# The last two batches' gate and val products by seven block products instead of eight, in a fused sigmoid attention and SwiGLU kernel

## The chip, the cores and the metric

The kernel runs on one core of one Trainium2 chip. TensorE multiplies matrices out of SBUF into PSUM (eight banks of 128 x 512 fp32), ScalarE (ACT) applies functions, VectorE (DVE) does arithmetic on tiles, GpSimd (POOL) casts and issues some transfers, and SyncE (SP) issues most of them. Each engine works its instructions in order; semaphores tie the engines together. The metric is the time on the device in microseconds (us), lower is better.

## What is computed

Eight batches of attention with 12 heads of 448 positions and 64 columns, where a sigmoid takes the place of the softmax, and then a SwiGLU block on the 3584 resulting rows of 768 columns:

```python
scores = scale * q @ k.T - log(S)            # per batch and head, S = 448
attn = 1 / (1 + exp(-scores))
x = (attn @ v)  -> rows (batch, position), 12 * 64 = 768 columns
g = x @ w_gate                               # 768 x 1536
val = x @ w_val                              # 768 x 1536
out = (g * sigmoid(g) * val) @ w_out         # 1536 x 768
```

Inputs and outputs are fp32; the kernel works in bf16 and fp16 with fp32 sums.

## The kernel before

**Attention.** 24 steps `i`: three groups of four heads for each of eight batches. For each step q, k and v are loaded by SP (`load`, 448 KB each), cast by GpSimd, q and k transposed by a transfer (`tr_dma`, from step 6 on) into a `qkT` tile, of which there are three. `burst` computes a pair of score tiles, `sig` the sigmoid of each on ScalarE into a `pt` tile, and `pv` the product with v, seven pairs a step. VectorE copies its result into `xT` tiles (two 128 x 448 tiles a step, six a batch).

**First FFN product (`f1`).** For each batch and each of 12 column blocks of 128, the gate and the val product: six 128 x 128 blocks of weights against six `xT` tiles. Two column blocks are worked together, each weight block as four 64 x 64 quarters (`quarters`, L511), so that different quarters of the array work on different products. ScalarE takes the sigmoid of gate, VectorE multiplies twice and puts the result into `hT` (two batches a tile), and with that frees the banks.

**Second FFN product (`f2_set`, `f2_pair`, `f2_single`).** It takes two batches together (pair `m`, 0 to 3), in sets of two blocks of 128 rows; each set is already worked by seven block products in place of eight. The sums of weight blocks that this needs are formed once (`weight_sums`). Two products are worked together in quarters while the steps go on; after them they are worked whole (`f2_single`, L678).

**What sets the order.** The kernel doesn't leave the order to the framework. Every piece of work is recorded as an `Op` with an engine, an assumed duration, what it depends on, and the buffers that it takes and gives. `list_schedule` (L70) then plays these through and gives each engine the order in which its instructions are written: on each engine the first operation that is ready among the next ones in the recorded order (40 for TensorE and VectorE, 30 for ScalarE, 8 for GpSimd, 1 for SP, so SP keeps the recorded order). A buffer ring is ready when the user of its slot before is done, by the planner's clock. For transfers that clock adds the assumed times on one common queue, and 1.7 us for the landing (`LAT["SP"]`). The order is fixed when the kernel is built; on the chip each engine waits wherever its next instruction isn't ready.

The recording loop (L872) goes through the steps and four slots in each. It hands out `f1` column blocks by `nf` (about four a step, behind attention by `LAG`), and `f2` items by `f2acc` (12.5 / 22 a slot). Loads for step i+3 are issued behind the transposes for step i+2. What is left of `f1` and `f2` when the steps are over is worked in a row.

Of the kernel before, what the change touches and what calls it, by code (L numbers as in the profile page):

```python
# [9 lines left out]
FP32 = mybir.dt.float32  # L10
FP16 = mybir.dt.float16
BF16 = mybir.dt.bfloat16
COPY = mybir.ActivationFunctionType.Copy
SIGM = mybir.ActivationFunctionType.Sigmoid
MULT = mybir.AluOpType.mult
ADD = mybir.AluOpType.add
SUB = mybir.AluOpType.subtract
# [10 lines left out]
class Op:  # L28
# [3 lines left out]
    def __init__(self, eng, dur, fn, deps=(), mode=("F", "F"), take=(), give=(), desc=(0, 0)):  # L32
        self.eng, self.dur, self.fn, self.mode = eng, dur, fn, mode
        self.deps = [d if isinstance(d, tuple) else (d, 0.0) for d in deps if d is not None]
        self.take = [Slot(t) for t in take]
        self.give = list(give)
        self.rank = self.t0 = self.t1 = None
        self.first = False
        n, size = desc
        self.hold = n == 1792  # L40
        self.dma = 2.0 if n == 1792 else n / 16 * max(0.042, size / 22300 - 0.003)
# [13 lines left out]
LAG = 1  # L55
# [8 lines left out]
TURN = "ACT"  # L64
WO = 4
MARGIN = 1.0
FREE = {"P"}


def list_schedule(ops, bufs, window):  # L70
# [113 lines left out]
def kernel(  # L184
# [10 lines left out]
    nc = tc.nc  # L195
# [19 lines left out]
    ctx.enter_context(tc.manual_schedule())  # L215

    slots = {"A": 2, "P": 8, "st": 11, "src": 2,
             "v16": 3, "qkT": 3, "pt": 10, "xT": 14, "osb": 3, "osf": 4, "S": 2, "t1": 3, "s16": 2}

    idn = one.tile([128, 128], BF16, tag="idn", name="idn")  # L220
    sb_t = one.tile([128, 1], FP32, tag="sbiast", name="sbiast")
# [33 lines left out]
    def op(*a, **kw):  # L255
        o = Op(*a, **kw)
        ops.append(o)
        return o

    def bank(name, n=0):  # L260

        return psum.tile([128, 512], FP32, tag=f"P{R['now'].got('P')[n].n}", bufs=1, name=name)

    def cp(eng, o, i):
        if eng == "ACT":
# [177 lines left out]
    def sig(key, dep, slot):  # L443
        def fn(a):
            def go():
                if a == 0:
                    T[("pt",) + key] = sb.tile([128, 2, S], FP16, tag="pt", bufs=slots["pt"], name="pt")
                nc.scalar.activation(out=T[("pt",) + key][:, a], in_=T[("sc",) + key][a][:, 0:S], func=SIGM, bias=sbias,  # L448
                                     scale=qkscale)
            return go  # L450
        x = op("ACT", 0.44, fn(0), deps=[dep], take=["pt"], give=slot[1:2])
        R["pt ring", key] = x.take
        R["sig"] = R[("pt",) + key] = op("ACT", 0.44, fn(1), deps=[x and (x, LAT["ACT"] + LATE)], give=slot[:1] + slot[2:])

    def pv(i):

# [72 lines left out]
    def f1(b, f):  # L529

        two = (f, f + 1)
        m, o = divmod(b, 2)

        def both(w, nm, parts, p):
            def fn():
                if p == 0:
                    for n, x in enumerate(two):
                        T[nm, b, x] = bank("ps_" + nm, n)[:, 0:S]
                quarters([[(T[nm, b, x], w[x // FC][:, j, (x % FC) * 128:(x % FC + 1) * 128], T["xT", b, j]) for x in two]
                          for j in range(*parts[p][1:])], parts, p, (nm, b, f))  # L540
            return fn

        def fs(f):
            def fn():
                t = T["s16", b, f] = sb.tile([128, S], FP16, tag="s16", bufs=slots["s16"], name="s16")
                nc.scalar.activation(out=t, in_=T["g", b, f], func=SIGM)  # L546
            return fn

        def ft(f):
            def fn():  # L550
                t = T["t1", b, f] = sb.tile([128, S], FP16, tag="t1", bufs=slots["t1"], name="t1")
                nc.vector.tensor_tensor(out=t, in0=T["g", b, f], in1=T["s16", b, f], op=MULT)  # L552
            return fn

        def fh(f):
            def fn():
                if o == 0 and f == 0:
                    T["hT", m] = sb.tile([128, NF, 2 * S], FP16, tag="hT", bufs=2, name=f"hT_{m}")
                nc.vector.scalar_tensor_tensor(  # L559
                    out=T["hT", m][:, f, o * S:(o + 1) * S], in0=T["v", b, f], scalar=HSC,  # L560
                    in1=T["t1", b, f], op0=MULT, op1=MULT)
            return fn
        xs = [(R["xT", b, j], 0.19 * j) for j in range(KC)]
        old = R["f2", m - 2] if m >= 2 and b % 2 == 0 else []

        def joint(w, nm, deps):
            a = None
            parts = [(0, 0, KC), (1, 0, KC)]
            if (b, f) == (0, 0) and nm in SPLIT:
                parts = [(0, 0, 4), (1, 0, 4), (1, 4, KC), (0, 4, KC)]  # L570
            ws = [(x, 0.38 * n) for c in {x // FC for x in two} for n, x in enumerate(R["w16", "w" + nm, c])]
            for p, (t, j0, j1) in enumerate(parts):
                same = p and parts[p - 1][0] == t
                a = op("PE", 0.19 * (j1 - j0), both(w, nm, parts, p), mode=("Q", "Q"), take=[] if p else ["P", "P"],
                       deps=[(x, 0.19 * n) for n, (x, _) in enumerate(xs[j0:j1])] + deps + ws +
                       [a and ((a, LAT["PE"] + LATE) if same else turn(a, (nm, b, f, p - 1)))])
                banks = banks if p else a.take
            return a, banks
        g, gbank = joint(wg16, "g", [])
        ts = []  # L580
        for n, x in enumerate(two):
            s = op("ACT", 0.45, fs(x), deps=[g], take=["s16"])
            s.first = 2
            ts.append(op("DVE", 0.54, ft(x), deps=[s], take=["t1"], give=s.take + gbank[n:n + 1]))

        def val():
            v, vbank = joint(wv16, "v", old + [(g, 1.0)])
            if f == NF - 2:
                v.give += [x for o, _ in xs for x in o.take]
            for n, (x, t) in enumerate(zip(two, ts)):  # L590
                R["hT", b, x] = op("DVE", 0.54, fh(x), deps=[v, t] + old, give=vbank[n:n + 1] + t.take)
        return val

    def weight_sums():

# [264 lines left out]
    def f1_step(b, f):  # L860
# [4 lines left out]
        if b % 2 == 1 and f == NF - 1:  # L865
            f2q.extend(f2_items(b // 2))

    f2acc = 0.0
    wsums = weight_sums()
    next(wsums)  # L870
    fpos = 0
    for i in range(NQ + QB + 2):  # L872
        att = i < NQ
        for sl in range(4):
            if i < QB:
                nf = 0
            elif i < QB + 4:
                nf = 1 if sl < 3 else 0
            else:
                nf = min(2, max(0, 4 * (i - QB) + sl - LAG - fpos + 1))  # L880
            if i < NCW and sl == 3:
                cast_wc(i)
            if WO < i <= WO + 4 and sl == 1:
                for f in range(3 * (i - WO - 1), 3 * (i - WO)):
                    cast_wo(f)
            if i > WO + 5 or i == WO + 5 and sl > 1:
                for _ in range(WSN):
                    next(wsums, None)
            f1s = []
            while len(f1s) < nf and fpos < B * NF and ("xT", fpos // NF, KC - 1) in R:  # L890
                f1s.append(divmod(fpos, NF))
                fpos += 1
            later = bursts(i, sl)
            for ds in later[:1 if i >= SPREAD else 2]:
                burst(ds)
            if sl == 0 and QB < i <= NQ:
                pv(i - 1)
            if sl == 0 and 0 < i < QB:
                pv(i - 1)
            if sl == 3 and i == QB - 1:  # L900
                pv(i)
            if att and i + 1 < NPE and sl in (1, 2):
                tr_pe(i + 1, sl - 1)
            for b, f in f1s:
                f1_step(b, f)
            for ds in later[1:] if i >= SPREAD else []:
                burst(ds)
            if att and sl == 0 and i + 2 < NQ:
                casts(i + 2)
            if att and sl == 1 and NPE <= i + 2 < NQ:  # L910
                tr_dma(i + 2)
            if sl == 1:
                if AHEAD <= i + 3 < NQ:
                    loads(i + 3)
                if WO <= i < WO + 4:
                    for f in range(3 * (i - WO), 3 * (i - WO + 1)):
                        load_wo(f)
                    uses[1] = uses[0]
            f2acc = f2acc + 12.5 / 22.0 if f2q else 0.4
            while f2q and f2acc >= f2q[0][0] and ("ws", 4, NH - 2) in R:  # L920
                w, fn = f2q.pop(0)
                f2acc -= w
                fn(not att)
    while fpos < B * NF:
        b, f = divmod(fpos, NF)
        fpos += 1
        f1_step(b, f)
    while f2q:
        f2q.pop(0)[1](True)

    window = {"PE": 40, "ACT": 30, "DVE": 40, "POOL": 8, "SP": 1}
    end = 0.0
# [39 lines left out]
```

## Time and profile before

| | |
|---|---|
| three runs | 406.99, 407.3, 410.8 us, median 407.3 |
| span of the profiled execution, first to last instruction | 407.6 us (0.3 above the median of the runs) |
| TensorE busy | 400.1 us, 98% |
| VectorE busy | 230.0 us, 56% |
| ScalarE busy | 223.2 us, 55% |
| GpSimd busy | 132.7 us, 33% |
| granted TensorE clock, mean | 0.997 of full speed |
| last score product of attention | about 333 us |
| whole output products at the end | 375.7 to 403.2 us |

The page shows the busy time of each engine, the span in 40 slices with the busy share of each in tenths, the transfers, the chain of work that ended last, and the groups of instructions that cost most. PE is TensorE, PEld its weight loads, DVE VectorE. A line like `L522 PE MATMUL ps_g<-xT,wg 64*64 64x448 x2304` is a group: source line, engine, the tile written and the tiles read, the shape, and how many. The time between matmuls is read from the chain in order of time rather than from their busy time, since matmuls overlap in the array.

### The profile page before, as it was taken

To read this page: it belongs to the slowest core of one execution; us is meant where nothing else is said; L and a number is where in the kernel's file an instruction comes from. 1 tells how busy PE (TensorE), PEld (TensorE's weight loads), DVE (VectorE), ACT (ScalarE), POOL (GpSimd) and SP (SyncE) were. 2 spreads that over 40 slices of the span, in tenths; PEclk is the share of its full clock that TensorE was granted. 3 is DMA by queue.
4 is the path that set the end of the run, shared out by engine and by line. 5 is a ranking of instruction groups with operands and counts; after the bars stand their busy time and mean duration, and the time that the engine had idled before them with its cause. 6 is when DMAs were issued, how large, how long until landed. Compare 5 with 4: busy or idle time off the path is not lost.

```text
span 407.6 us, 17541 instructions
## 1 busy us (share of the span) xinstructions
PE 400.1 (98%) x7871; PEld 306.8 (75%) x7873; DVE 230.0 (56%) x420; ACT 223.2 (55%) x472; POOL 132.7 (33%) x194
## 2 busy tenths in 40 slices
PE   8999999999999999999999999999999999999995
PEld 3446667668998787665679888889989898997663
DVE  2624544447795467553564664745465656546874
ACT  4997677757767743377647456475474552121100
POOL 1888855656454221522332322422310200000000
PEclk9999999999999999999999999999999999999998
DMA  7999999999676609455665564663500303010335
GB/s 268 380 376 376 376 277 318 304 320 264 184 185 183 160 26 203 139 129 108 209 183 92 172 136 143 177 133 122 124 4 3 80 2 77 7 42 18 101 85 148
DMA packets 64795, 67.58 MB, mean 166 GB/s; under 512 B 35536, under 2 KB 60880, under 8 KB 64720
## 3 DMA queue, kind: packets, MB, share of 16 engines
q1 hardware_dynamic: 62864, 59.78, 51.6%
q0 software_dynamic: 1536, 6.29, 6.0%
q8 instruction: 61, 1.00, 1.0%
q10 hardware_dynamic: 320, 0.39, 0.3%
q14 instruction: 14, 0.11, 0.1%
HBM read 47.19 MB, written 11.01 MB: 143 GB/s over the span
## 4 chain that ended last, share of the span: by engine, by line
PE 95%; ACT 2%; DMA 1%; issue 1%; DVE 0%; ACTq 0%
PE ps_v L522 27%; PE ps_g L522 27%; PE ps_o L522 16%; PE ps_sc L427 8%; PE ps_pv L468 7%; PE ps_o L678 7%; ACT pt L448 2%; PE ps_warm L818 1%; PE ps_tr L384 1%; DMA st<-in_q_dram 1%; DVE st L687 0%; DVE src L268 0%; ACTq L504 0%
## 5 line engine op out<-in xcount | busy, mean ns | idle before, releaser
L448 ACT ACTIVATE pt<-ps_sc 128x448 f16<-128x448 f32 x336 | 162.7, 550 | 77.8 <-PE ps_sc L427 77.3
L522 PE MATMUL ps_v<-xT,wv 64*64 64x448 f16 x2304 | 136.2, 349 | 0.0
L522 PE MATMUL ps_g<-xT,wg 64*64 64x448 f16 x2304 | 134.6, 349 | 0.8 <-issue 0.6
L522 PEld LDWEIGHTS <-wg 64*64 64x64 f16 x2304 | 93.7, 107 | 22.2 <-issue 2.4
L522 PEld LDWEIGHTS <-wv 64*64 64x64 f16 x2304 | 93.2, 107 | 21.2 <-issue 1.4
L552 DVE TENSOR_TENSOR t<-ps_g,s 128x448 f16<-128x448 f32 x96 | 56.5, 618 | 71.6 <-ACT s L546 71.6
L546 ACT ACTIVATE s<-ps_g 128x448 f16<-128x448 f32 x96 | 48.1, 545 | 59.0 <-PE ps_g L522 50.0
L559 DVE SCALAR_TENSOR_TENSOR hT<-ps_v,t 128x448 f16<-128x448 f32 x96 | 55.4, 618 | 43.4 <-PE ps_v L522 26.2
L427 PE MATMUL ps_sc<-qkT 64*64 64x448 bf16 x672 | 77.2, 354 | 0.1
L270 POOL CAST src<-st 128x896 bf16<-128x896 f32 (+1 forms) x43 | 40.8, 951 | 64.5 <-DMA st<-in_q_dram 35.8
L270 POOL CAST v<-st 64x448 f16<-64x448 f32 (+1 forms) x72 | 41.5, 577 | 60.0 <-PE ps_pv L468 42.5
L522 PEld LDWEIGHTS <-hT 64*64 64x64 f16 x1080 | 52.2, 107 | 7.0 <-issue 0.2
L522 PE MATMUL ps_o<-wo,hT 64*64 64x384 f16 x648 | 49.2, 323 | 0.0
L522 PE MATMUL ps_o<-st,s 64*64 64x384 f16 x480 | 45.7, 323 | 0.0
L468 PE MATMUL ps_pv<-pt,v 64*64 64x448 f16 x672 | 45.3, 350 | 0.1
L522 PE MATMUL ps_o<-st,hT 64*64 64x384 f16 x432 | 41.2, 323 | 0.0
L427 PEld LDWEIGHTS <-qkT 64*64 64x64 bf16 x672 | 33.7, 107 | 9.9 <-issue 1.6
L687 DVE SCALAR_TENSOR_TENSOR osb<-ps_o,osb 128x384 f32<-128x384 f32 x63 | 32.9, 550 | 10.4 <-PE ps_o L522 6.6
L268 DVE CAST xT<-ps_pv 128x448 f16<-128x448 f32 x40 | 23.6, 617 | 25.0 <-PE ps_pv L468 25.0
L697 POOL DMA_DIRECT2D out_dram<-osb x32 | 16.7, 526 | 59.0 <-DVE osb L687 59.0
L468 PEld LDWEIGHTS <-v 64*64 64x64 f16 x672 | 26.6, 107 | 9.1 <-issue 2.7
L522 PEld LDWEIGHTS <-s 64*64 64x64 f16 x480 | 29.1, 107 | 3.8 <-issue 0.4
(44 smaller groups left out, 212.8 us busy)
## 6 DMA issues: line engine op xcount, KB each, us to landing
st<-in_q_dram SPq DMA_DIRECT2D x24, 448.0 KB, 5.0
st<-in_v_dram SPq DMA_DIRECT2D x24, 448.0 KB, 6.6
st<-in_k_dram SPq DMA_DIRECT2D x23, 448.0 KB, 5.9
out_dram<-osb POOLq DMA_DIRECT2D x32, 192.0 KB, 3.3
st<-in_moe_w_gate_dram SPq DMA_DIRECT2D x12, 384.0 KB, 8.8
st<-in_moe_w_val_dram SPq DMA_DIRECT2D x12, 384.0 KB, 8.8
st<-in_moe_w_out_dram SPq DMA_DIRECT2D x12, 384.0 KB, 7.6
out_dram<-st SPq DMA_DIRECT2D x16, 192.0 KB, 2.8
```

What stands on the lines that cost most here:

```text
L268: nc.vector.tensor_copy(out=o, in_=i)
L270: nc.gpsimd.tensor_copy(out=o, in_=i)
L427: nc.tensor.matmul(out=sc[a][64 * (g ^ a):64 * (g ^ a) + 64, 0:S].rearrange("k (s p) -> k s p", s=NS), lhsT=kT[r, s, 64 * g:64 * g + 64], ...
L448: nc.scalar.activation(out=T[("pt",) + key][:, a], in_=T[("sc",) + key][a][:, 0:S], func=SIGM, bias=sbias, scale=qkscale)
L468: nc.tensor.matmul(out=T["pv", i, a][64 * g:64 * g + 64, :], lhsT=T["v16", i][r, a, s, :], rhs=T["pt", i, s][r, a, :], start=(s == 0), sto ...
L522: mm = nc.tensor.matmul(out=o[cs], lhsT=w[rs, cs], rhs=x[rs], start=p == 0 and k == 0, stop=p == len(parts) - 1 and k == len(steps) - 1)
L546: nc.scalar.activation(out=t, in_=T["g", b, f], func=SIGM)
L552: nc.vector.tensor_tensor(out=t, in0=T["g", b, f], in1=T["s16", b, f], op=MULT)
L559: nc.vector.scalar_tensor_tensor(out=T["hT", m][:, f, o * S:(o + 1) * S], in0=T["v", b, f], scalar=HSC, in1=T["t1", b, f], op0=MULT, op1=MULT)
L678: nc.tensor.matmul(out=T["p", m, k, n], lhsT=lhs()[:, x // 2, x % 2], rhs=rhs(x), start=x == 0, stop=x == NH - 1)
L687: nc.vector.scalar_tensor_tensor(out=c(*dst), in0=T["p", m, k, n], scalar=HREC, in1=c(*other), op0=MULT, op1=ADD)
L697: dma.dma_start(out=out[rows, cols].rearrange("(p s) d -> s p d", s=NS)[s], in_=T[("osb",) + t][64 * x:64 * x + 64, cols])
```

## The change

Batches 6 and 7 (pair 3) leave `f1`. Once the last attention step is recorded, their gate and val products are worked by six sets, one for each pair of column blocks (f, f + 6), by seven products of half the inner size in place of eight. Each product is a whole 128 x 128 tile times three, not in quarters.

- `f1_sums` forms four combinations of weight blocks for each set and for gate and val by VectorE, from step 13 on, one such group every third slot. All groups use one buffer (`TT`). `store` writes each to DRAM from SP; it is recorded when the next group is.
- `wload` brings them back after attention into the staging buffers, five ahead.
- `xsum` forms combinations of `xT` tiles by VectorE when attention is done.
- `one_set` issues the seven products for gate and val in turn. Results that several outputs share stay in the bank, and ScalarE takes a copy (`snap`) between two products that add onto it. SILU by ScalarE takes the place of the sigmoid and one multiplication. All SILUs come behind the last sigmoid.
- The ring of `qkT` tiles has two in place of three; `pt` has 9, now handed out by the planner in any order, and `xT` 16 in place of 14.
- The first six batches' `f1` blocks are handed out at four a step up to nine steps past the third, then at 3.2; `f2` items at 0.42 a slot (0.6 after the last `f1` block). Two items of pair 2 are recorded after each set, the last three behind the sets.

```diff
-FREE = {"P"}
+FREE = {"P", "pt", "W"}
+NPLAIN = 6
+RATE = 0.42
+FR = 3.2
+F0 = 9
+RATE2 = 0.6
+KEEP = 3
+TW0 = 13
+TSTEP = 3
+MIX = 2
...
-             "v16": 3, "qkT": 3, "pt": 10, "xT": 14, "osb": 3, "osf": 4, "S": 2, "t1": 3, "s16": 2}
+             "v16": V16, "qkT": 2, "pt": PT, "W": NEARLY0, "TT": 1, "xT": XT, "osb": 3, "osf": 4, "S": 2, "t1": 3, "s16": 2}
...
+    def f1_sums(nm, f):
+
+        w = wg16 if nm == "g" else wv16
+        t = []
+
+        def q(k):
+            return t[0][:, k]
+
+        def fn(k, x, y):
+            def go():
+                if k == 0:
+                    t.append(sb.tile([128, 4, NC, 128], FP16, tag="TT", bufs=1, name=f"tt_{nm}{f}"))
+                nc.vector.tensor_tensor(out=q(k), in0=x(), in1=y(), op=SUB)
+            return go
+        b = {(r, c): (lambda r=r, c=c: blk(w, f, r, c)) for r in range(2) for c in range(2)}
+        ws = [x for c in (f // FC, (f + NH) // FC) for x in R["w16", "w" + nm, c]]
+        o = [op("DVE", 0.36, fn(0, b[0, 1], b[0, 0]), deps=ws, take=["TT"])]
+        o.append(op("DVE", 0.36, fn(1, b[1, 1], lambda: q(0)), deps=[o[0]]))
+        o.append(op("DVE", 0.36, fn(2, b[1, 1], b[0, 1]), deps=[o[1]]))
+        o.append(op("DVE", 0.36, fn(3, b[1, 0], lambda: q(1)), deps=[o[2]]))
+
+        def store():
+            R["T", nm, f] = [op("SP", 0.5, lambda: nc.sync.dma_start(
+                out=tsum[NH * "gv".index(nm) + f], in_=t[0].rearrange("p k j f -> p (k j f)")), deps=[o[3]],
+                give=o[0].take, desc=(128, 4 * NC * 256))]
+        return store
...
+        def wload(nm, f):
...
+            old = [R["cq", NQ - 1][-1], R["ck", NQ - 1][-1]] + [R["v16", i] for i in (NQ - 2, NQ - 1)]
+            WS[k] = op("SP", 0.5, fn, deps=old + R["T", nm, f], take=["W"], desc=(128, 4 * NC * 256))
...
+                for j in range(NC):
+                        nc.tensor.matmul(out=T["fp", key], lhsT=win(nm, f, n)()[:, j], rhs=xin[n](j),
+                                         start=n in first and j == 0, stop=j == NC - 1,
+                                         skip_group_check=n not in first)
...
+            both(1, lambda nm: [last] if last else [R["xT", b1, j] for j in range(KC)])
+            for nm in "gv":
+                snap(nm, 1)
+            both(2)
+            add("g", 0, 0, 2, 1, True)
+            silu(0, 0)
+            both(6, lambda nm: [C[nm, "s", 1]])
+            for nm in "gv":
+                snap(nm, 6)
+            add("v", 0, 0, 2, 1, True)
+            fin(0, 0)
+            both(5)
+            both(7, lambda nm: [C[nm, "s", 6]])
+            for nm in "gv":
+                snap(nm, 7)
+            add("g", 1, 1, 5, 7, False)
+            silu(1, 1)
+            add("v", 1, 1, 5, 7, False)
+            both(4, lambda nm: [C[nm, "s", 7]])
+            silu(1, 0)
+            fin(1, 0)
+            fin(1, 1)
+            both(3, lambda nm: [C[nm, 1, 1]])
+            add("g", 0, 1, 3, 6, True)
+            silu(0, 1)
+            add("v", 0, 1, 3, 6, True)
+            fin(0, 1)
+            return P["v", 7]
...
+            if i >= TW0 and (4 * i + sl) % TSTEP == 0:
+                if tstores:
+                    tstores.pop()()
+                if tpairs:
+                    tstores.append(f1_sums(*tpairs.pop(0)))
...
-            while len(f1s) < nf and fpos < B * NF and ("xT", fpos // NF, KC - 1) in R:
+            while len(f1s) < nf and fpos < NPLAIN * NF and ("xT", fpos // NF, KC - 1) in R:
...
-            f2acc = f2acc + 12.5 / 22.0 if f2q else 0.4
-            while f2q and f2acc >= f2q[0][0] and ("ws", 4, NH - 2) in R:
+            f2acc = f2acc + (RATE2 if fpos == NPLAIN * NF else RATE) if f2q else 0.4
+            while len(f2q) > (KEEP if fpos == NPLAIN * NF else 0) and f2acc >= f2q[0][0] and ("ws", 4, NH - 2) in R:
                 w, fn = f2q.pop(0)
                 f2acc -= w
-                fn(not att)
-    while fpos < B * NF:
...
+                fn(False)
+            if i == NQ and sl == 3:
+                sums, wload, one_set = f1_pair(B // 2 - 1)
+                sums()
+                todo = [(nm, f) for f in range(NH) for nm in "gv"]
+                for x in todo[:5]:
+                    wload(*x)
+                last = None
+                for f in range(NH):
+                    last = one_set(f, last)
+                    for _ in range(min(MIX, len(f2q) - KEEP)):
+                        f2q.pop(0)[1](False)
+                    for x in todo[5 + 2 * f:7 + 2 * f]:
+                        wload(*x)
     while f2q:
-        f2q.pop(0)[1](True)
+        f2q.pop(0)[1](False)
+    for _, fn in f2_items(B // 2 - 1):
+        fn(True)
```

## The prediction

> **What bounds the kernel now.** I read in the order: the page's busy shares and slices, the chain of work that ended last, the stretches of time, then the queue of transfers.
>
> ```profile
> PE 400.1 (98%) x7871; PEld 306.8 (75%) x7873; DVE 230.0 (56%) x420; ACT 223.2 (55%) x472; POOL 132.7 (33%) x194
> ...
> PE   8999999999999999999999999999999999999995
> ...
> PE 95%; ACT 2%; DMA 1%; issue 1%; DVE 0%; ACTq 0%
> ```
>
> TensorE is the chain: 95% of it, and busy in every slice but the first and the last. So a product that goes is worth its own time, and any wait that TensorE gets is a loss of the same size. Nothing else is near a limit by its share (VectorE 56%). What a product costs stands in the chain in order of time, near the end (start, length, what):
>
> ```profile
> 371.13 1.14 PE ps_g L522 x24
> 372.26 1.14 PE ps_v L522 x24
> 373.40 1.08 PE ps_o L678 x6
> 374.48 1.26 PE ps_v L522 x24
> 375.74 27.42 PE ps_o L678 x168
> ```
>
> 24 quarter matmuls are six 128x128 weight blocks over 448 columns: 1.136 us, 0.1893 us a block. 168 whole matmuls of 384 columns take 27.42 us, 0.1632 each, so 0.1904 for 448 columns. A change between quarters and whole tiles costs 1.08 - 6 x 0.163 = 0.10 us one way and 1.26 - 1.14 = 0.12 us back, 0.11 on average.
>
> [...]
>
> **Part 1, products removed.** Batches 6 and 7 now take 2 batches x 12 column blocks x 2 (gate, val) x 6 = 288 blocks in quarters, 288 x 0.1893 = 54.5 us. After: 6 sets x 2 x 7 products x 3 = 252 whole blocks, 252 x 0.1904 = 48.0 us. Gain 6.5 us, all on the chain.
>
> **Part 2, mode changes.** In the order built from the changed kernel the last stretch (after attention) changes between quarters and whole tiles 23 times, because half pairs of output products fill the gaps of the sets; before it is 3 times. 20 x 0.11 = 2.2 us lost.
>
> **Part 3, work around the new sets.** A set costs TensorE 14 x 0.57 = 8.0 us. ScalarE: 6 snapshots and 4 SILUs at 0.55 us (the sigmoid rows, 550 and 545 ns) = 5.5 us. VectorE: 7 reads of PSUM at 0.62 us and 3 products in SBUF at about 0.35 = 5.4 us. Both are covered by TensorE. Tightest step: product 7 of gate ends, 0.2 us to ScalarE, snapshot 0.45 to 0.55, 0.15 back, and product 4 of gate stands 1.1 us behind product 7 (val's lies between): 0.2 to 0.3 us to spare. If that cover is gone it costs at most some 1 us a set, 6 us in all; I take 0.3 us for the part. The 12 sums of xT blocks lie under 8.1 us of products. The table load (row: ACT_TABLE_LOAD 1283 ns) lies in the 2.5 us in which ScalarE waits for product 2. The reloads from DRAM are issued a set ahead. The tail is the same.
>
> So far: -6.5 + 2.2 + 0.3 = -4.0 us.
>
> **Part 4, the weight sums during attention.** 48 subtractions of 128x384; the row L664 of 128x768 takes 0.55 us, so between 0.28 (half) and 0.42 (the 128x512 copy); I take 0.33, 16 us of VectorE in some 110 us. VectorE is busy 7.5 us of each 13 there now (nine stretches from 141 to 259 us): room enough. But the four blocks of a set share one buffer (`TT`, one slot): the first subtraction of each set waits until the *store of the set before has landed*, and VectorE stops in order until then. Queued behind it are the reads that free PSUM banks (`t1`, `hT`, `osb`), and TensorE waits for those.
>
> When does the store land? It is issued on SP behind the transpose and three loads. With two qkT buffers, transpose i+2 waits for the last score product of step i (before, with three, of step i-1; its qkT is wanted a step of 13 us later and lands in 4 to 7.5, so that itself costs nothing). So end of scores, transpose, q, k, v, store. Stretch 150 to 285 us (queue view: size, median time to landing), and one such turn:
>
> ```profile
> st<-in_q_dram SPq DMA_DIRECT2D x8, 448.0 KB, 4.3
> st<-in_k_dram SPq DMA_DIRECT2D x8, 448.0 KB, 5.4
> st<-in_v_dram SPq DMA_DIRECT2D x8, 448.0 KB, 6.2
> qkT<-src SPq DMA_TRANSPOSE x9, 5.8
> ```
>
> ```profile
> 220.22 3.82 SPq L410 DMA_TRANSPOSE qkT<-src  x1
> 224.09 0.59 SPq L300 DMA_DIRECT2D st<-in_q_dram  x1
> 224.72 0.49 SPq L300 DMA_DIRECT2D st<-in_k_dram  x1
> 225.26 0.47 SPq L300 DMA_DIRECT2D st<-in_v_dram  x1
> ```
>
> Here v is issued 5.0 us after the transpose and lands 6.5 later: 11.55 us. The eight turns from 154 to 270 us give 12.1, 8.3, 12.0, 9.5, 11.55, 9.7, 9.1, 10.85. Add 0.3 from the last score to the transpose's issue, 1.0 for 384 KB more in the queue (consecutive w_out loads land 1.0 apart) and 0.1 to wake VectorE: the store lands 9.7 to 13.5 us after the step's last score, mean 11.8. The kernel's planner believes 9.3 (transpose 2.5 us, loads 1.24 each, store 1.08, landing 1.7, from its constants), and puts the waiting subtraction there: in the built order it stands just behind reads of products that end 8 to 9 us after that score.
>
> How late may it start? I walked the built order: for each of these waits, the first TensorE instruction whose semaphore needs a VectorE instruction queued behind it, its distance (sum of products, in the times above) from the step's last score, less the VectorE work between (0.33, 0.6 and 0.51 us each) and 0.15 us. Example, val sums of block 0: last score at 155.0 us of product time, score product 4940 at 166.5 needs `t1` behind one subtraction (latest start 165.4), and the pv product at 167.8 needs `hT` behind four (165.1). Allowance 10.1 us. Eight waits stand so, with allowances of 10.1, 9.8, 10.5, 10.0, 10.5, 10.2, 10.2 and 10.5 us. The other three wait for stores issued behind no loads; they have 0 to 0.3 us too little, 0.5 us in all.
>
> Landing less 10.2: 3.3, 0, 3.2, 0.7, 2.8, 0.9, 0.3, 2.1, mean 1.7 us a wait. With the four turns before 150 us (emptier queue: 1.0, 0, 0.2, 1.2) it is 1.3. Eight waits: 10 to 13 us; I take 10.5 + 0.5 = 11 us. Bounds: all turns like the shortest, 0; all like the longest, 8 x 3.3 + 1.5 = 28. TensorE doesn't get it back: it has no idle time to give. In 150 to 285 us of before the VectorE reads end a median 1.3 us ahead of the TensorE instruction that needs them, and one unforeseen wait of 1.5 us at 170 us cost nothing; that speaks for the lower half of 0 to 28.
>
> [...]
>
> **Sum.** 407.6 (span of the profiled execution) - 4.0 + 11 = 414.6 us. The median of the three runs is 407.3, 0.3 below that span: 414.3.
>
> **Rivals.** *A, forecast: the products go, the store's wait takes more back*, 408 to 422 us. For it: eight turns of which seven exceed the allowance. Against: transfers in the after run may be less crowded, since output products come slower (fewer stores from POOL in each turn).
>
> *B, the waits are harmless: faster.* Stores land by about 10 us as in the turns of 8.3 and 9.1 us, or banks have more to spare than the walk says. 407.3 - 4.0 = 403.3, down to 401 if the mode changes hide behind other waits. For: the harmless wait at 170 us. Decides below some 0.4 us a wait.
>
> *C, waits eat just the gain*: 0.3 to 1 us a wait, 403 to 411 us, within 1%.
>
> *D, transposes late*: with two qkT buffers a score burst waits for its transpose. Landing 4 to 7.5 us of a 13 us step leaves over 5 us; it decides only if the turn before slips by that. If it did, 1 to 2 us in each of 18 steps: 425 to 440. Unlikely.
>
> **Chances.** A with D: slower by over 1% (above 411.4 us) 0.60; C: within 1% 0.25; B: faster by over 1% (below 403.2) 0.15. One per cent is about what a measurement of this kernel can tell from no change. Range 402.5 to 422: from B, less the 0.3 us of part 3 and some of the mode changes, to eight waits of 2.2 us each (the mean of the six longest turns): 407.3 - 4.0 + 17.4 + 0.5 = 421.2.
>
> **What would show it.** Right: from 150 us on, VectorE's subtractions idle 1 to 3 us each for the DMA of `tsum`, about eleven times; the slices of TensorE between the 14th and the 28th drop from 9 to 8; attention's last score comes 8 to 13 us later than the products alone allow; the last stretch has whole products at 0.19 us a block without gaps, and some 23 mode changes. Wrong: subtractions that wait as long while TensorE shows no idle time (banks to spare), or that hardly wait (stores land sooner); or gaps between the products of a set, ahead of product 7 or 4, waiting for ScalarE.

## The result, and the profile after

The changed kernel takes 421.51 us (median of four runs, 419.89 to 424.62), the kernel before 408.14 beside it: 1.033 times the time, 95% interval 1.027 to 1.039. The forecast was 414.3 us, slower, with a range of 402.5 to 422. The time lies just inside the range. The direction and the mechanism were right and the size was not: 7 us more were forecast and 13.4 came.

The page of the changed kernel, the lines that answer to those shown of before:

```profile
span 422.8 us, 15909 instructions
...
PE 401.5 (95%) x6973; PEld 267.4 (63%) x6973; DVE 249.9 (59%) x492; ACT 244.5 (58%) x509; POOL 134.6 (32%) x202
...
PE   8999989999999999998979898699999999999995
...
PEclk9999999999999999999989999879999999999999
...
PE 72%; DMA 13%; DVE 6%; SPq 4%; ACT 3%; issue 1%; DVEq 0%; ACTq 0%
```

TensorE was the chain with 95%; now it holds 72%, and transfers 13%. Its slices fall below 9 between the 19th and the 26th, which is 190 to 275 us, inside the stretch in which the waiting groups of weight sums are made (181 to 303 us). After that it is full again. The granted clock, which I hadn't thought of, falls too, in the 21st, 26th and 27th slice.

What ends VectorE's idle time before a group's first subtraction, between 150 and 320 us (us in total, times, longest):

```profile
DVE tt_g L640 <- DMA tsum<-tt_v: 14.3, 4, 6.8
DVE tt_v L640 <- DMA tsum<-tt_g: 12.1, 5, 4.0
```

So the first subtraction of a group of sums stands nine times for the store of the group before, 26.4 us in all. VectorE in order of time (start, length, ..., idle time before it and what ended it), the two worst:

```profile
212.45 0.59 DVE L640 TENSOR_TENSOR tt_v<-wv,wv 128x384 f16<-128x384 f16 x1 [3.96 <-DMA tsum<-tt_g]
...
274.50 0.55 DVE L640 TENSOR_TENSOR tt_g<-wg,wg 128x384 f16<-128x384 f16 x1 [6.81 <-DMA tsum<-tt_v]
```

TensorE in order of time, just behind each:

```profile
214.73 1.71 PE L492 MATMUL ps_pv<-pt,v 64*64 64x448 f16 x16 [2.53 <-DVE osb L908]
...
275.57 0.59 PE L449 MATMUL ps_sc<-qkT 64*64 64x448 bf16 x4 [4.96 <-DVE osb L908]
```

The wait doesn't stop TensorE by itself. It stops the read of a bank (`osb`) queued behind the subtraction, and TensorE waits for that bank: a pause of 2.53 us stands behind the wait of 3.96, and one of 4.96 behind that of 6.81.

**Where the 13.4 us come from.** I count, for each matmul, its start less the sum of the spacings of all matmuls before it (the rows of the prediction: 0.0473 us for a quarter of 448 columns, 0.1904 for a whole one, and so on). While TensorE runs without a gap this number stands still; what it grows by is lost. From 120 us to attention's last score product it grows by 1.3 us in the kernel before and by 20.3 in the changed one: 19.0 lost. From there to the end it grows by 0.2 and by 2.5: 2.3 for the mode changes. The products that went are worth 6.5. That is 407.6 - 6.5 + 2.3 + 19.0 = 422.4, against a span of 422.8.

The last stretch went as forecast. The chain in order of time there (start, length, what):

```profile
333.10 2.07 PE ps_o L546 x48
335.17 0.67 PE ps_g L723 x3
335.85 0.57 PE ps_v L723 x3
336.42 0.57 PE ps_g L723 x3
```

A product of three blocks takes 0.57 us without a gap behind it. Where the mode changes it takes 0.67, and 48 quarters of 384 columns take 2.07 in place of 48 x 0.0406 = 1.95: 0.10 and 0.12 us a change.

### The profile page after: what moved, and what is told of

Same layout as the page of the kernel before. It is cut to its first block, busy times and chain, and to the rows that moved or that the text cites. A ratio compares the mean times of both kernels' runs of the same rounds, so it can differ in the third digit from the quotient of the medians.

```text
span 422.8 us, 15909 instructions
## 1 busy us (share of the span) xinstructions
PE 401.5 (95%) x6973; PEld 267.4 (63%) x6973; DVE 249.9 (59%) x492; ACT 244.5 (58%) x509; POOL 134.6 (32%) x202
## 4 chain that ended last, share of the span: by engine, by line
PE 72%; DMA 13%; DVE 6%; SPq 4%; ACT 3%; issue 1%; DVEq 0%; ACTq 0%
PE ps_v L546 15%; PE ps_g L546 13%; PE ps_o L546 12%; DMA tsum<-tt_v 7%; PE ps_o L899 7%; PE ps_g L723 6%; PE ps_pv L492 6%; PE ps_sc L449 6%; PE ps_v L723 6%; DMA tsum<-tt_g 5%; ACT pt L470 2%; SPq L322 2%; SPq L432 2%; PE ps_warm L1039 1%; DVE tt_v L640 1%
## 5 line engine op out<-in xcount | busy, mean ns | idle before, releaser
L546 PE MATMUL ps_v<-xT,wv 64*64 64x448 f16 x1728 | 102.6, 354 | 0.0
L546 PE MATMUL ps_g<-xT,wg 64*64 64x448 f16 x1728 | 99.2, 349 | 1.5 <-issue 1.1
L546 PEld LDWEIGHTS <-wv 64*64 64x64 f16 x1728 | 63.1, 109 | 23.8 <-issue 1.5
L546 PEld LDWEIGHTS <-wg 64*64 64x64 f16 x1728 | 61.7, 107 | 25.1 <-issue 3.1
L576 DVE TENSOR_TENSOR t<-ps_g,s 128x448 f16<-128x448 f32 x72 | 42.9, 618 | 44.6 <-ACT s L570 44.4
L918 POOL DMA_DIRECT2D out_dram<-osb x40 | 20.8, 525 | 115.2 <-DVE osb L908 105.5
L583 DVE SCALAR_TENSOR_TENSOR hT<-ps_v,t 128x448 f16<-128x448 f32 x72 | 41.7, 617 | 23.7 <-PE ps_v L546 16.7
L570 ACT ACTIVATE s<-ps_g 128x448 f16<-128x448 f32 x72 | 36.5, 548 | 24.2 <-PE ps_g L546 18.2
L449 PEld LDWEIGHTS <-qkT 64*64 64x64 bf16 x672 | 30.4, 107 | 23.4 <-issue 13.5
L908 DVE SCALAR_TENSOR_TENSOR osb<-ps_o,osb 128x384 f32<-128x384 f32 x70 | 36.6, 549 | 8.3 <-PE ps_o L546 7.9
```

What stands on the lines that cost most here:

```text
L449: nc.tensor.matmul(out=sc[a][64 * (g ^ a):64 * (g ^ a) + 64, 0:S].rearrange("k (s p) -> k s p", s=NS), lhsT=kT[r, s, 64 * g:64 * g + 64], ...
L546: mm = nc.tensor.matmul(out=o[cs], lhsT=w[rs, cs], rhs=x[rs], start=p == 0 and k == 0, stop=p == len(parts) - 1 and k == len(steps) - 1)
L583: nc.vector.scalar_tensor_tensor(out=T["hT", m][:, f, o * S:(o + 1) * S], in0=T["v", b, f], scalar=HSC, in1=T["t1", b, f], op0=MULT, op1=MULT)
L908: nc.vector.scalar_tensor_tensor(out=c(*dst), in0=T["p", m, k, n], scalar=HREC, in1=c(*other), op0=MULT, op1=ADD)
```

## The experiments

All edits are to the changed kernel, but for the memsets, which go into the kernel before. The waits are read from 120 us on. The growth is the number above, from 120 us to attention's last score. "Half clock" is the time between 100 and 380 us in which the granted clock is 0.5.

| run | VectorE's waits for a store, us | growth, us | half clock, us | time, us |
|---|---|---|---|---|
| before | - | 1.3 | 0 | 407.4 to 408.4 |
| the change | 26.4 | 20.3 | 10.2 | 421.5 |
| one group of sums | 0 | 1.3 | 0 | 403.7 |
| belief +2 us | 9.7 | 5.7 | 0 | 408.3 |
| belief +4 us | 0 | 4.8 | 0 | 409.2 |
| store from ScalarE's queue | 11.1 | 13.4 | 3.4 | 416.7 |
| one group a step, from step 10 | 32.6 | 25.9 | 10.2 | 427.4 |
| two slots | 21.4 | 18.0 | 6.8 | 420.2 |
| three `qkT` tiles | 23.4 | 17.7 | 6.8 | 421.3 |
| belief +4 us, one group a step, from step 10 | 3.9 | 2.4 | 0 | 404.3 |

**One group of sums: what the rest of the change is worth.** The other eleven groups and their stores are left out; every reload takes the first group.

```diff
-                nc.sync.dma_start(out=T["W", nm, f].rearrange("p k j f -> p (k j f)"), in_=tsum[NH * "gv".index(nm) + f])
+                nc.sync.dma_start(out=T["W", nm, f].rearrange("p k j f -> p (k j f)"), in_=tsum[0])
...
-            WS[k] = op("SP", 0.5, fn, deps=old + R["T", nm, f], take=["W"], desc=(128, 4 * NC * 256))
+            WS[k] = op("SP", 0.5, fn, deps=old + R["T", "g", 0], take=["W"], desc=(128, 4 * NC * 256))
...
-    tpairs = [(nm, f) for f in range(NH) for nm in "gv"]
+    tpairs = [("g", 0)]
```

> The changed kernel with eleven of the twelve groups of weight sums and their stores left out; every reload after attention takes the one group that is formed (so the products of batches 6 and 7 use wrong sums). What is left is the price of the seven products, the mode changes, the rings and the hand-out rates. Theory: -6.5 us of products, +2.2 of mode changes, +0.3: 403 to 405 us, and TensorE without a pause from 100 us on. Rival (transposes a step later, or the slower hand-out, cost by themselves): 410 us or more.

403.71 us against 407.39 of the kernel before, ratio 0.991 (95% interval 0.988 to 0.993, here and below): 3.7 us won, where the prediction's parts 1 to 3 came to 4.0. The loss lies in the sums and their stores.

**The planner's belief.** The planner counts a store as landed 1.7 us after its place in the common queue of transfers. Here it adds 4.0 us for these stores alone. The instructions are the same, and only their order changes.

```diff
+        self.late = 0.0
...
-                    o.t1 = dma + LAT["SP"]
+                    o.t1 = dma + LAT["SP"] + o.late
...
+            R["T", nm, f][0].late = 4.0
```

> The changed kernel with one thing altered: the planner believes that each store of a weight-sum group lands 4 us later than before. The work is the same; VectorE's subtractions are merely written later in its order. Theory (VectorE waits for the store's landing, TensorE pays, and its clock halves in the longer pauses): VectorE's idle time for the stores falls from 26 us to below 6, TensorE's loss between 190 and 310 us from 19.5 us to below 4, and the time from 421.5 to 403 to 407 us. Rival (the loss comes from 16 us more work on VectorE and from the transposes issued a step later, and the waits are only where it shows): 415 us or more.

409.16 us, ratio to before 1.004 (1.002 to 1.007). The page:

```profile
PE   8999999999999999999999999999999999999995
...
PEclk9999999999999999999999999999999999999999
```

No subtraction waits for a store any more, and the dips of TensorE and of its clock are gone: 12 of the 13.4 us come back. It misses the expected 403 to 407. Attention's growth is 4.8 us in place of the 1.3 with one group of sums, and behind attention's last score there are 31 mode changes in place of 23 and the growth is 4.9 in place of 2.5. The last group's sums come only at 293 us; that this is what costs the rest is not shown by this run.

With 2.0 in place of 4.0:

> The planner believes a landing 2.0 us later instead of 4.0. Theory (each group pays what its landing comes later than believed, over an allowance): the nine waits of the change, 26.4 us together, lose up to 2 us each, some 9 to 12 us remain, and no pause is long enough for TensorE to fall to half clock: 409 to 414 us. Rival (the 4.0 us helped by another order of the last stage, 62 changes of tile mode and later sums, and not by the waits): the order is nearly that of the change (48 changes in the planner's order), so 418 us or more.

408.28 us, ratio 0.999 (0.995 to 1.002). The waits fell to 9.7 us as the theory has it, and the last stretch has the 23 mode changes of the change, and yet the time is far below the rival's 418. It is also below the 409 expected. So two microseconds of belief bring as much as four.

**The store from another queue.** The store is issued by ScalarE, so that no transpose or load stands ahead of it on SP and it holds none.

```diff
-            R["T", nm, f] = [op("SP", 0.5, lambda: nc.sync.dma_start(
+            R["T", nm, f] = [op("ACT", 0.5, lambda: nc.scalar.dma_start(
```

> The changed kernel with the twelve stores of weight sums issued by ScalarE in place of SyncE, so that they no longer stand behind a transpose and three loads. Theory: a store lands some 3 to 5 us after the sums; VectorE waits next to nothing; ScalarE pays 12 x 0.5 to 1.2 us of issuing, beside its other work. 403 to 408 us. Rival (it is the one buffer and the landing itself, not the queue ahead of it, or the extra work of VectorE): above 412 us.

416.68 us, ratio 1.022 (1.020 to 1.025): the expectation fell. The queue of ScalarE and, in another view, VectorE in order of time:

```profile
154.19 0.36 ACTq L650 DMA_DIRECT2D tsum<-tt_g  x1
```

```profile
162.15 0.36 DVE L640 TENSOR_TENSOR tt_v<-wv,wv 128x384 f16<-128x384 f16 x1 [4.81 <-DMA tsum<-tt_g]
```

SP had issued three loads of 448 KB between 149.8 and 153.1 us. The store, on a queue of its own, still frees the slot only 8.0 us after its issue: in this run a queue of its own didn't bring that store in early. Waits of 11.1 us remain, and not all of them behind loads: the second store, ahead of which SP had issued nothing since 153.1 us, landed 2.3 us after its issue, and VectorE still stood 2.91 us for it, since ScalarE, in its own order, issued it only at 171.87 us, more than 5 us after the group's last subtraction.

**Memsets in place of the waits.** The kernel before, with 8, 16, 32 and 4 memsets put into VectorE's order in the attention steps: the delay alone, with no sums and no stores.

```diff
+    HELD = [(190.0, 8), (225.0, 16), (260.0, 32), (295.0, 4)]
...
+        if o.eng == "DVE" and HELD and o.t0 > HELD[0][0]:
+            for _ in range(HELD.pop(0)[1]):
+                nc.vector.memset(wide, 0.0)
```

> The kernel before, with VectorE kept busy by memsets of a scratch tile at four places that the planner doesn't know of: 8 memsets at about 205 us (some 1.6 to 2.2 us), 16 at about 240, 32 at about 275, 4 at about 310. Theory: TensorE loses the delay less some 1.3 us of spare banks: 0.5, 2.5, 6 and 0 us; in the pauses above some 2.5 us its granted clock falls to a half and stays there for 3.4 or 6.8 us, which adds 1.7 to 3.4 us each. Together 10 to 16 us over 408. Rival (banks absorb such waits, and the pauses after the change had another cause): below 3 us.

426.92 us in one run, 19.5 over the kernel before, above the 10 to 16 expected. The memsets took VectorE 3.01, 6.15, 12.41 and 1.45 us, and TensorE lost 4.0, 3.3, 12.6 and 0. So at these four places a delay of 1.45 us is covered and one of 3 us or more is not, and the 3 us cost more than the 6. The stretches of the trace show why (TensorE's busy time is the first number behind the length, then the other engines; the granted clock stands behind POOL's):

```profile
187.56:190.98 3.42, 1.53 (x18) 0.70 (x18) 2.58 (x10) 2.32 (x6) 0.00 (x0) 1.00 0.20 39
190.98:194.39 3.41, 3.41 (x40) 2.22 (x43) 1.41 (x3) 0.98 (x2) 1.03 (x2) 0.50 1.03 206
225.11:228.52 3.41, 1.89 (x40) 1.50 (x32) 2.33 (x10) 1.96 (x4) 1.67 (x3) 1.00 1.04 229
228.52:231.94 3.42, 2.19 (x46) 1.75 (x49) 2.47 (x6) 0.00 (x0) 1.84 (x2) 1.00 0.79 295
269.49:272.90 3.41, 0.00 (x0) 0.00 (x0) 2.40 (x9) 0.00 (x0) 0.00 (x0) 1.00 0.00 0
272.90:276.30 3.40, 0.00 (x0) 0.00 (x0) 2.49 (x9) 0.00 (x0) 0.00 (x0) 0.50 0.00 0
```

After the first delay TensorE idled 1.89 us of one 3.41 us window, and ran the next window, with 3.41 us of work, at half clock (0.50): by estimate 1.7 us more, half of 3.41. The second delay gave a longer pause, 2.58 us, but split over two windows (1.52 and 1.23 us of idle time), and the clock stayed at 1.00 in both.

**Fewer groups in a stretch.** The groups start at step 10 and come once a step, with the change's own belief.

```diff
-TW0 = 13
-TSTEP = 3
+TW0 = 10
+TSTEP = 4
```

> The groups of sums start at step 10 and come once every four quarter steps, and the planner's belief about the landing is the change's own. Theory (the planner's belief is what counts: it gives VectorE the next subtraction some 9.3 us after the step's last score, the slot comes free 10 to 16 us after it, however far apart the groups are meant to be): six or more waits of 1 us or more on a store remain, and 407 to 416 us. Rival (twelve groups in 110 us are too many for one slot, and one group in a step is not): hardly a wait, 402 to 405.5 us.

427.4 us, ratio 1.044 (1.038 to 1.050), above even what the theory expected: ten waits, 32.6 us. Spacing the groups out does not help while the planner places each subtraction where it believes the slot free.

**Two slots.** Two `TT` buffers; `pt` 8 and `t1` 2 make room.

```diff
-PT = 9
+PT = 8
...
-             "v16": V16, "qkT": 2, "pt": PT, "W": NEARLY0, "TT": 1, "xT": XT, "osb": 3, "osf": 4, "S": 2, "t1": 3, "s16": 2}
+             "v16": V16, "qkT": 2, "pt": PT, "W": NEARLY0, "TT": 2, "xT": XT, "osb": 3, "osf": 4, "S": 2, "t1": 2, "s16": 2}
...
-                    t.append(sb.tile([128, 4, NC, 128], FP16, tag="TT", bufs=1, name=f"tt_{nm}{f}"))
+                    t.append(sb.tile([128, 4, NC, 128], FP16, tag="TT", bufs=slots["TT"], name=f"tt_{nm}{f}"))
```

> Two slots for a group's sums in place of one; to make room for it, 8 in place of 9 buffers of the scores after the sigmoid and 2 in place of 3 of the product of the sigmoid and gate. The planner's belief is the change's own. Theory (VectorE stands for the one slot): no wait for a store over 1 us, since the store before the last has landed more than 10 us earlier, and 403 to 408 us, with what the smaller buffers cost. Rival (the stores on SP hold the next step's transpose, and their traffic delays the loads): the transposes still land late and the time stays at 414 us or more.

420.21 us, ratio 1.029 (1.024 to 1.034). My theory that VectorE stands for the single slot fell. VectorE in order of time:

```profile
127.15 0.34 DVE L640 TENSOR_TENSOR tt_g<-wg,wg 128x384 f16<-128x384 f16 x1
...
142.37 0.35 DVE L640 TENSOR_TENSOR tt_v<-wv,wv 128x384 f16<-128x384 f16 x1
...
183.11 0.53 DVE L640 TENSOR_TENSOR tt_g<-wg,wg 128x384 f16<-128x384 f16 x1 [0.62 <-DMA tsum<-tt_g]
...
198.94 0.36 DVE L640 TENSOR_TENSOR tt_v<-wv,wv 128x384 f16<-128x384 f16 x1 [2.28 <-DMA tsum<-tt_v]
```

SP in order of time:

```profile
173.04 1.51 SPq L432 DMA_TRANSPOSE qkT<-src  x1
...
176.83 1.25 SPq L650 DMA_DIRECT2D tsum<-tt_g  x1
```

The first group is summed from 127 us on and stored only at 176.83, because SP keeps the recorded order and the store is recorded in step 13. The second slot lets the sums run one group further ahead of a store that hasn't moved. From the third group on seven of ten wait for a store again; their place in the order is the moment in which the planner believes that it landed. It bought depth and no time.

**Three `qkT` tiles, as before the change.** `xT` 14 and `pt` 8 make room. The transposes, and what stands behind them on SP, then go out a step earlier.

```diff
-XT = 16
-PT = 9
+XT = 14
+PT = 8
...
-             "v16": V16, "qkT": 2, "pt": PT, "W": NEARLY0, "TT": 1, "xT": XT, "osb": 3, "osf": 4, "S": 2, "t1": 3, "s16": 2}
+             "v16": V16, "qkT": 3, "pt": PT, "W": NEARLY0, "TT": 1, "xT": XT, "osb": 3, "osf": 4, "S": 2, "t1": 3, "s16": 2}
```

> Three qkT tiles as before the change in place of two, with 14 in place of 16 xT tiles and 8 in place of 9 pt buffers to make room; the planner's belief about the landing is the change's own. The transposes, and the loads and the store behind them, now go out about a step earlier, in belief as on the chip. Theory (the error of the belief about what lies between transpose and landing is what costs): the belief errs as before, so VectorE still stands 10 us or more in all for stores, and 413 to 424 us (some 1 us more for 62 instead of 48 changes of tile mode). Rival (the cut of the qkT ring is the cause, since the transpose then waits for the step's last score and everything behind it is late): under 5 us of such waits, and 403 to 409 us.

421.3 us, ratio 1.029 (1.024 to 1.035), with 23.4 us of waits. The cut of the ring isn't the cause: a store that goes out earlier is also believed earlier.

**The version that wins.** The later belief, and one group a step from step 10, so that the last sums come at 273 us: the two edits above together.

> The planner believes a landing of the stores of sums 4.0 us later, as in the run with that edit alone (409.2), and the groups of sums start at step 10 instead of 13 and come once every four quarter steps instead of every three. What cost the change time was VectorE standing at a group's first subtraction. Theory (only the planner's belief about the landing and the lateness of the last sums cost the rest): no wait of VectorE for a store over 1 us, the last sums done by 275-285 us, TensorE never at half clock between 150 us and the end, and 402 to 405.5 us, the time of the run with one group of sums (403.7). Rival (the 48 sums' own 17 us on VectorE and the stores' traffic cost time wherever they stand): 407 us or more, as with the later belief alone.

404.59 us, ratio 0.989 (0.983 to 0.995). Once more, with more runs:

> The later belief and the earlier, sparser sums once more, with more runs beside the kernel before: 403.5 to 405.5 us, a ratio of 0.985 to 0.995.

404.29 us against 408.34, ratio 0.992 (0.989 to 0.994): faster than both kernels, and by its ratio level with the run with one group of sums (0.991). Its page:

```profile
span 403.5 us, 15914 instructions
...
PE   8999999999999999999999999999999999999995
...
PE 92%; DMA 3%; ACT 2%; issue 1%; DVE 1%; ACTq 0%
```

and its one wait for a store:

```profile
DVE tt_g L641 <- DMA tsum<-tt_v: 3.9, 1, 3.9
```

TensorE is the chain again, with 92%. The rival of the first of these runs, that the 48 sums cost time wherever they stand, falls. The expectation of no wait over 1 us missed too: one of 4.6 us stood in the first run and this one of 3.9 in the second. But it cost TensorE only some 0.6 us, where the wait of 3.96 us in the change cost 4.3 with the clock. So the length of a wait alone doesn't give its cost.

Last, up to six output items behind each set in place of two (`MIX = 6`), for fewer mode changes:

> The later belief and the earlier, sparser sums, and up to 6 instead of 2 of the waiting output groups are put behind each set of seven products, so that the planner's order changes the tile mode 44 times instead of 48. If a change of mode costs 0.1 us, 0.4 us less than without it, which the runs can hardly tell; if it costs 0.2 us or more, as the last stage of the run with the later belief alone suggested (2.4 us for 12 changes more), 0.8 us less or more.

404.48 us, ratio 0.991 (0.988 to 0.994): no difference that can be told. The last stretch has 19 changes in place of 23 and grows by 2.0 in place of 2.5 us, 0.12 a change. The run with the later belief alone has eight changes more behind attention's last score, not twelve as the expectation says: some 1.0 of the 2.4 us by which its last stretch grew more. The rest are waits there, the longest 0.63 us for a snapshot of ScalarE.

## Why the prediction's mechanism was right and its size wrong

**What bounds the kernel**: right. Every loss above shows as idle time, half clock or mode changes of TensorE.

**Parts 1 to 3**, -6.5 + 2.2 + 0.3: right. The run with one group of sums measures them together, -3.7 for -4.0; the mode changes cost 2.3, and the sets of the change have no gaps.

**Part 4**: the mechanism was right, and the size of its sum is the step that failed: 11 us taken, 19 measured. The wait, the queue behind it and the belief of the planner are those of the prediction; the two runs with a later belief show the cause, since nothing but the order changed there. The allowance of 10.2 us holds roughly: landing less 10.2 gives 16.7 us, and TensorE lost 14.0. The seven stores that I took to stand behind a transpose and three loads, in order (landing, or the start of the subtraction where that waited, counted from the step's last score, and what TensorE lost in pauses; the fourth landed before its subtraction's turn):

| | 1 | 2 | 3 | 4 | 5 | 6 | 7 | sum |
|---|---|---|---|---|---|---|---|---|
| landing, us | 10.3 | 12.6 | 13.2 | 10.2 | 14.2 | 11.4 | 16.2 | |
| less 10.2 | 0.1 | 2.4 | 3.0 | 0 | 4.0 | 1.2 | 6.0 | 16.7 |
| TensorE lost | 0 | 2.4 | 2.8 | 0 | 2.3 | 1.3 | 5.2 | 14.0 |

Three terms were too small:

- *The landing.* I had 9.7 to 13.5 us, mean 11.8, less a little because four early turns were shorter: 1.3 us a wait. It was 10.2 to 16.2, mean 12.6, and TensorE lost 2.0 us a store: 14.0 in place of 10.5. The turns that I read were of the kernel before, which has no such stores, and I added one constant for the store. The two longest lie outside my range. SP in the longest of them, in order of time:

```profile
258.52 3.90 SPq L432 DMA_TRANSPOSE qkT<-src  x1
262.46 1.48 SPq L322 DMA_DIRECT2D st<-in_q_dram  x1
263.98 0.75 SPq L322 DMA_DIRECT2D st<-in_k_dram  x1
264.83 0.64 SPq L322 DMA_DIRECT2D st<-in_v_dram  x1
265.51 0.57 SPq L650 DMA_DIRECT2D tsum<-tt_v  x1
```

  The transpose takes 3.90 us to issue, as in the turn of before that I showed (3.82), but then the store needs 9.0 us more until VectorE runs at 274.50, where I had 7.5. What the traces show of it: GpSimd issued four output stores between 257.96 and 259.50 us, around the transpose, and the transpose landed only 10.2 us after its issue. The transfers issued between 257.9 and 259.6 us (size, median time to landing) and, in another view, the transpose of the fourth turn, issued at 212.31 us:

```profile
out_dram<-osb POOLq DMA_DIRECT2D x4, 192.0 KB, 6.5
qkT<-src SPq DMA_TRANSPOSE x1, 10.2
```

```profile
qkT<-src SPq DMA_TRANSPOSE x1, 4.0
```

  The three turns without such a store in flight are the three shortest of the seven (10.3, 10.2 and 11.4 us), the four with two or more the longest. So the output stores, which the prediction expected to be fewer and named only as a point against, look like a part of what spread the landings. No run tests it, and it isn't the whole: with 2 us of belief one store landed 8.4 us after its issue with no output store ahead of it.
- *The last groups*, whose stores I took to stand behind no loads: 1.8 us in place of 0.5. One of the three, issued at 283.83 us, does stand behind a transpose and three loads (277.73 to 281.98), and the wait for it makes 1.1 of the 1.8.
- *The clock*: not in the prediction at all. TensorE lost some 1.5 and 1.9 us while it ran at half clock after the two pauses shown above (the granted clock is 0.5 for 3.41 us from 214.65 us on and for 6.83 us from 272.68 on): 3.4 us. Stretches around the second (columns as with the memsets):

```profile
270.00:273.00 3.00, 0.62 (x15) 0.15 (x5) 0.00 (x0) 1.47 (x4) 1.68 (x2) 0.95 0.85 311
273.00:276.00 3.00, 0.43 (x8) 0.28 (x11) 1.50 (x4) 0.00 (x0) 1.68 (x3) 0.50 0.02 8
276.00:279.00 3.00, 3.00 (x44) 2.02 (x40) 3.00 (x8) 0.98 (x2) 0.00 (x0) 0.50 0.32 120
```

  The three together: 11 + 3.5 + 1.3 + 3.4 = 19.2.

**The rivals.** B and C needed less than 1 us a wait; it was 2.1 (19.2 for nine), the clock with it. D, that a score burst waits for its transpose, doesn't show: each wait of TensorE that the profile lists between 150 and 320 us ends with VectorE. The point "one unforeseen wait of 1.5 us cost nothing, that speaks for the lower half" was a poor witness: the memsets agree that 1.45 us cost nothing, and show that 3 us cost 4. And the signs that I named were too mild: nine waits of 0.7 to 6.8 us, not eleven of 1 to 3, and attention's last score 21.5 us later than in the run with one group of sums (319.1 against 297.6), not 8 to 13.

## What to carry to other kernels

Where an order is fixed by a planner, an instruction that waits for a transfer is as late as the planner's error about that transfer, and everything queued behind it on its engine is late with it (VectorE stood 26.4 us for the stores in the change, 9.7 with 2 us of later belief and 0 with 4). More buffers, another queue or more distance helped little or not at all here as long as the planner kept its error (a second slot won 1.3 of the 13.4 us, ScalarE's queue 4.8, and one group a step lost 5.9 more); tell the planner the landing that the trace shows, and then start the work early enough for the later belief. When TensorE is the chain, read the granted clock around each of its pauses too: at the change's pauses of 2.53 and 4.96 us it stood at 0.5 for 3.41 and 6.83 us, and TensorE lost some 1.5 and 1.9 us more by that.

## What the runs showed of the chip

In two runs the half-clock stretches begin a whole number of 3.413 us apart: with the memsets at 190.98 and 272.90 us, 24 x 3.413; in the change at 214.65 and 272.68, 17 x 3.413. In the change they last 3.41 and 6.83 us, one and two such windows; with the memsets the longest takes three, from 272.90 to 283.13 us.

Counted in windows of that length from these starts, TensorE in the change idled 2.45 us in the window ahead of the first stretch, 2.06 in the one ahead of the second, and 2.89 in the second's own first window, which another at half clock followed. In every other window of the change between 150 and 320 us it idled 1.31 us or less, and the next one ran at full clock (1.00). With the memsets, 1.89 and 3.41 us of idle time in a window were followed by half clock; 1.52 us were not, and the next window, with 1.23, ran at 1.00. One window at half clock is of another kind: TensorE idled only 0.24 us in the window ahead of it. It comes after the longest memsets, where two windows without any work lie ahead of that (same columns, and the window that follows it):

```profile
276.31:279.72 3.41, 3.17 (x30) 1.62 (x33) 3.38 (x8) 0.98 (x2) 1.03 (x2) 0.50 0.00 0
279.72:283.13 3.41, 3.41 (x44) 2.61 (x39) 0.37 (x2) 0.75 (x2) 0.00 (x0) 0.50 0.48 115
```

So in these two runs, where TensorE ran at full clock before, half clock went not with the length of a pause but with how much of it fell into one window: 1.89 us in one cost clock, and a pause of 2.58 us over two did not.
